# Sliding-window attention into an ELU feed-forward: four more groups transposed on TensorE, a split last chunk, and a new order of issue

## The chip, the core and the metric

The kernel runs on one core of one Trainium2 chip. The metric is the device time of one execution in microseconds (us); lower is better. A core has five engines that run their own instruction streams and meet only at semaphores: TensorE (PE; its weight loads are listed apart as PEld), VectorE (DVE), ScalarE (ACT), GpSimd (POOL) and SyncE (SP). Transfers are issued from the streams of SP, POOL and ACT and are carried by 16 DMA engines which all of them share.

## The reference

```python
scores = scale * np.matmul(q, k.transpose(0, 1, 3, 2))      # q, k, v: 8 x 8 x 576 x 64
mask = np.abs(pos[:, None] - pos[None, :]) <= 32
scores = np.where(mask, scores, -1000000000.0)
scores = scores - np.max(scores, axis=-1, keepdims=True)
attn = np.exp(scores)
attn = attn / (np.sum(attn, axis=-1, keepdims=True) + 1e-09)
attn_out = np.matmul(attn, v)
x = attn_out.transpose(0, 2, 1, 3).reshape(4608, 512)
h = x @ w_in                                                # w_in: 512 x 2048
g = np.where(h > 0.0, h, np.exp(np.minimum(h, 0.0)) - 1.0)
out = g @ w_out                                             # w_out: 2048 x 512
```

Inputs and output are fp32. Matmul operands on the chip are bf16, sums are fp32.

## The kernel before

**Units, groups, tiles, chunks.** The 8 x 576 query rows are cut into 72 units of 64 rows, nine to a batch. Attention works on groups of one or two units (list `G`; groups 0 to 8 cover units 0 to 15, and group i from 9 on covers units 2i-2 and 2i-1). The feed-forward works on tiles t of 2, 2, 2, 3, 4, 3 units and then seven tiles of 8 units (512 rows); tile 6 is made of groups 9 to 12, tile 7 of groups 13 to 16. Its output is made in 36 chunks c of 128 rows.

**What one group does.** Its queries and keys must stand transposed in SBUF, its values as blocks. Step `L` loads rows from DRAM (SP), `C`/`CV` cast them to bf16 (POOL; some of batch 0 on ACT and DVE), `TT` transposes k and q by a DMA (SP) from batch 2 on; batches 0 and 1 use TensorE (`T`, `TR`, with copies `TT` and `TTR` out of PSUM). Then `QK` (TensorE) makes the scores, `SM` (ACT) their exponential, `MK` (DVE) the mask, `AV` in two halves (TensorE) the product with v, `RN` (DVE) divides by the row sum and leaves x of the group in `xs`. From group 13 on, every second group is a "twin": its scores are made in the same `QK` step as those of the group before it, in the banks psT and psH.

**x must be transposed before the feed-forward.** Function `X` (L531) has two ways. For groups below `NC0 = 9` four TensorE transposes write psT (L544; step `XT`), and step `X` copies psT to the tile `xt` on ACT or DVE (L313 or L315, called from `XE`). For the others one DMA issued by SP does it (L540; step `X`). All groups of a tile must be in `xt` before its first `H`.

**The feed-forward.** `H` (L568) is four matmuls (16 or 8 for the small tiles) into one of three psH banks; `EX` (ACT, L577) is the exponential; `FF` clips it, on ACT (L589) or DVE (L591); `GG` (DVE, L597 or L600) takes the maximum with h, writes g and frees the bank. For the 8-unit tiles `FF` is on ACT for three of four. `Y` (L615) has four parts of four matmuls for each chunk; `YC` (ACT, L621) copies the sum to SBUF and frees the bank, `OUT` (L625) stores it from ACT's queue. `ypool` (L602) says in which bank a chunk is summed: psY alone for the first six, then psY and psT in turn, and four banks in turn for the last four chunks.

**What sets the order.** No loop nest does. Each step is given to a planner (`Plan`, L21) with an engine, a cost, dependences, the buffers it takes and frees, and a due time ("rank": about 4.0 per unit) to which the table `SHIFT` adds a number for each step named there. The planner walks through time, always starts the ready step of lowest rank on a free engine, and thereby fixes the order of issue of every engine. Table `ENG` moves single steps between ACT and DVE (or POOL). During its first 26 us the planner puts short dummy matmuls (`fill`, L514) into the gaps that it foresees on TensorE. At run time the engines follow that order strictly, each instruction waiting for the semaphores of what it needs.

**The start.** SP loads the rows of batch 0. POOL waits for block v2 of batch 0 (`WAIT`, L309), and then issues the loads of the second half of batch 0 (`LR`, L388, four transfers), of the weights (`WI`, L688, and `WO`, L693, four quarters each), and of batch 1 (`LR` 1).

Of the kernel before, what the change touches and what calls it, by code (L numbers as in the profile page):

```python
# [8 lines left out]
FP32 = mybir.dt.float32  # L9
# [181 lines left out]
def kernel(  # L191
# [9 lines left out]
    nc = tc.nc  # L201

    B, H, S, D = q.shape
# [3 lines left out]
    DM = H * D  # L207
# [14 lines left out]

    NBR = 2
    NTA = 5
    NC0 = 9
    NXT = 3
    NTW = 13
    NMA = 5
# [15 lines left out]
    yp = ctx.enter_context(tc.tile_pool(name="yp", bufs=3))  # L244
    psS_p = ctx.enter_context(tc.tile_pool(name="psS", bufs=1, space=PSUM))
    psO_p = ctx.enter_context(tc.tile_pool(name="psO", bufs=1, space=PSUM))
    psT_p = ctx.enter_context(tc.tile_pool(name="psT", bufs=1, space=PSUM))
# [63 lines left out]
    def copy(eng, dst, src):  # L311
        if eng is nc.scalar:
            nc.scalar.copy(dst, src)  # L313
        else:
            eng.tensor_copy(dst, src)  # L315
# [234 lines left out]
        copy(eng, dst, pt)  # L550


    es, ys = {}, {}

    def gcols(t):
        c = tiles[t][0] * QB % GC
# [44 lines left out]

    def ypool(c):  # L602
        if c < NCH - 4:
            return ((psY_p, "psY"), (psT_p, "psT"))[c % 2 if c >= 6 else 0]
        return ((psY_p, "psY"), (psO_p, "psO"), (psT_p, "psT"),
                (psS_p, "psS"))[c % 4]

# [8 lines left out]
                             rhs=w_out_sb[:, fo, :],  # L616
                             start=(fo == 0), stop=(fo == NFO - 1))

    def YC(c):
        y = yp.tile([128, DM], FP32, name="y", tag="y")  # L620
        nc.scalar.copy(y, ys.pop(c))  # L621
        ys[c] = y

    def OUT(c):
        nc.scalar.dma_start(out[c * 128:c * 128 + 128, :], ys.pop(c))  # L625

    NCH = N_TOK // 128
    sizes = [2, 2, 2, 3, 4, 3] + [8] * 7
# [2 lines left out]
    for t, n in enumerate(sizes):  # L631
# [8 lines left out]
    PER = 4.0  # L640
    LL, CC, XX = 36, 18, 14
    ENG = {
        ("CV", 0, 0, 0): "POOL", ("X", 4): "DVE", ("FF", 0, 4): "DVE", ("FF", 1, 0): "ACT",
        ("FF", 1, 8): "ACT", ("FF", 1, 12): "DVE", ("FF", 2, 0): "ACT", ("FF", 2, 4): "DVE",
        ("FF", 3, 6): "DVE", ("FF", 3, 10): "DVE", ("FF", 4, 0): "ACT", ("FF", 4, 4): "ACT",
        ("FF", 4, 6): "DVE", ("FF", 4, 8): "ACT", ("FF", 5, 2): "DVE"}
    SHIFT = {
        ("WI", 0): -17, ("WI", 1): -21, ("LR", 0, "k", 0): -31, ("LR", 0, "k", 1): -30,
        ("LR", 0, "q", 0): -29, ("LR", 0, "q", 1): -40, ("WI", 2): -21, ("WI", 3): -22,
        ("WO", 1): -23, ("WO", 2): -21, ("LR", 1, "k", 0): 2, ("WO", 3): -4, ("L", 0, "k",  # L650
        0): -32, ("L", 0, "k", 1): -33, ("L", 0, "q", 0): -40, ("L", 0, "v", 0): -35, ("L",
        0, "k", 2): -36, ("L", 0, "q", 1): -43, ("L", 0, "v", 2): -40, ("L", 0, "v", 4):
        -40, ("L", 1, "v", 0): -114, ("L", 1, "v", 1): -114, ("L", 1, "v", 3): -105, ("L",
        1, "v", 4): -117, ("L", 2, "k", 0): -6, ("TT", 2, 0): -138, ("L", 2, "k", 1): -6,
        ("TT", 2, 1): -5, ("TT", 2, 2): -13, ("TT", 3, 0): -4, ("TT", 3, 2): -10, ("L", 3,
        "k", 3): -6, ("TT", 3, 3): -7, ("L", 3, "k", 4): -6, ("TT", 3, 4): -16, ("L", 4,
        "k", 0): -6, ("L", 4, "k", 1): -6, ("TT", 4, 2): -40, ("TT", 4, 3): 8, ("TT", 4, 4):
        -17, ("L", 5, "k", 2): -6, ("TT", 5, 2): -11, ("L", 5, "k", 4): -6, ("TT", 5, 4): 1,
        ("TT", 6, 0): -30, ("TT", 6, 1): -8, ("L", 6, "v", 2): -4, ("TR", 1, "k", 0): 166,
        ("TR", 1, "k", 1): 174, ("TR", 1, "k", 2): 168, ("TR", 1, "q", 0): 169, ("TR", 1,  # L660
        "q", 1): 191, ("TR", 1, "q", 3): 158, ("QK", 3): -64, ("QK", 5): 187, ("XT", 7): 13,
        ("AV", 8, 0): 11, ("XT", 8): 55, ("X", 9): 17, ("QK", 10): 46, ("AV", 10, 0): 32,
        ("AV", 10, 1): 88, ("X", 10): 14, ("RN", 11, 0): 60, ("X", 11): 7, ("X", 14): -10,
        ("X", 16): -48, ("X", 17): 17, ("X", 18): -3, ("X", 19): 10, ("SM", 20, 0): -48,
        ("SM", 22, 0): -43, ("AV", 22, 0): 77, ("AV", 22, 1): 104, ("QK", 23): 41, ("X",
        23): 15, ("H", 0, 12): 81, ("H", 2, 0): 117, ("H", 2, 12): -98, ("GG", 2, 12):
        -2044, ("H", 3, 0): 140, ("H", 3, 2): 81, ("H", 3, 8): 186, ("H", 3, 12): 141, ("H",
        3, 14): 103, ("H", 4, 0): -34, ("H", 4, 2): -22, ("H", 4, 4): -18, ("H", 4, 14): 33,
        ("H", 5, 0): 21, ("H", 5, 2): 39, ("H", 5, 4): 19, ("FF", 5, 4): 81, ("GG", 5, 4):
        63, ("H", 5, 6): 57, ("H", 5, 10): 84, ("H", 5, 12): 13, ("H", 6, 0): 104, ("H", 6,  # L670
        11): -162, ("H", 7, 4): -158, ("H", 7, 10): -73, ("H", 8, 3): -74, ("EX", 8, 8): 49,
        ("EX", 9, 5): 17, ("Y", 0, 3): 100, ("Y", 1, 0): 152, ("Y", 1, 2): 164, ("Y", 3, 1):
        111, ("Y", 4, 1): 30, ("Y", 4, 3): 41, ("Y", 5, 0): 57, ("Y", 8, 3): -75, ("Y", 9,
        1): -191, ("Y", 9, 2): -68, ("Y", 11, 0): -79, ("Y", 11, 2): -47, ("Y", 12, 1):
        -140, ("Y", 13, 1): -67, ("Y", 14, 1): 34, ("Y", 14, 3): 90, ("Y", 15, 0): 116,
        ("Y", 15, 2): -18}
    RING, XBT = 2.8, 1.33
    LEAD = 36.0

# [200 lines left out]
    for i in range(NG):  # L880
        r = prank(i)
# [100 lines left out]
    for c in range(NCH):  # L982
# [16 lines left out]
        deps = [("Y", c, NQ - 1)]  # L999
        if c >= 3:  # L1000
            deps.append(("OUT", c - 3))
        P.op(("YC", c), "ACT", 0.6, r, deps, lambda c=c: YC(c),
             rel=(ypool(c)[1], 1))
        P.op(("OUT", c), "ACT", 0.42, r, [("YC", c)],
# [34 lines left out]
```

## Time and profile before

| what | value |
|---|---|
| median of 5 runs | 321.97 us (320.23 to 324.64) |
| the profiled execution, its own time | 319.84 us |
| its span, first to last instruction | 318.10 us |
| PE busy / PEld busy | 306.6 us (96%) / 169.3 us |
| ACT busy / DVE busy / POOL busy | 211.0 / 193.4 / 113.8 us |
| queue 1 (SP's loads and transposes), share of 16 engines | 64.8% |
| DMA transposes of x (L540), k and q (L332) | 28, median 3.3 us to landing; 30, 4.3 us |
| mean granted TensorE clock | 0.995 |

"Busy" adds up the times in which an engine has an instruction in work. Matmuls overlap one another, so a busy PE can still lose time, and the spacing between starts says more than the duration of one. The same holds for ACT: an instruction listed at 0.60 us can be followed by the next after 0.5. The 1.74 us between the span and the execution's own time lie before the first and after the last instruction. Times in the views count from the start of the span.

### The profile page before, as it was taken

To read this page: it belongs to the slowest core of one execution; us is meant where nothing else is said; L and a number is where in the kernel's file an instruction comes from. 1 tells how busy PE (TensorE), PEld (TensorE's weight loads), DVE (VectorE), ACT (ScalarE), POOL (GpSimd) and SP (SyncE) were. 2 spreads that over 40 slices of the span, in tenths; PEclk is the share of its full clock that TensorE was granted. 3 is DMA by queue.
4 is the path that set the end of the run, shared out by engine and by line. 5 is a ranking of instruction groups with operands and counts; after the bars stand their busy time and mean duration, and the time that the engine had idled before them with its cause. 6 is when DMAs were issued, how large, how long until landed. Compare 5 with 4: busy or idle time off the path is not lost.

```text
span 318.1 us, 7590 instructions
## 1 busy us (share of the span) xinstructions
PE 306.6 (96%) x2935; PEld 169.3 (53%) x2935; DVE 193.4 (61%) x414; ACT 211.0 (66%) x358; POOL 113.8 (36%) x166
## 2 busy tenths in 40 slices
PE   7899999999999997999999999999999999999995
PEld 5578776477754443444444544444454545444442
DVE  5147956779765797484658656758474848444300
ACT  2359754679765987676878638788777786676711
POOL 4980029956652355564265656412100000000000
PEclk9799999999999999999999999999999999999999
DMA  8999999999999999999999999998611111100121
GB/s 166 206 207 207 207 223 224 254 195 216 201 201 214 194 181 199 214 213 204 205 234 192 242 188 192 220 174 180 141 50 53 49 52 49 52 33 33 61 74 66
DMA packets 153636, 51.42 MB, mean 162 GB/s; under 512 B 143104, under 2 KB 148992, under 8 KB 153600
## 3 DMA queue, kind: packets, MB, share of 16 engines
q1 hardware_dynamic: 142304, 35.53, 64.8%
q0 software_dynamic: 6112, 5.96, 11.4%
q10 hardware_dynamic: 5184, 9.44, 9.1%
q8 instruction: 23, 0.38, 0.5%
q14 instruction: 13, 0.11, 0.1%
HBM read 36.70 MB, written 9.44 MB: 145 GB/s over the span
## 4 chain that ended last, share of the span: by engine, by line
PE 80%; DMA 8%; ACT 4%; POOL 3%; DVE 2%; issue 1%; SPq 0%; ACTq 0%; POOLq 0%
PE psH L568 33%; PE psY L615 21%; PE psT L615 15%; DMA w_out_sb<-in_moe_w_out_dram 5%; PE psO L501 5%; DMA xt<-xs 2%; PE psS L444 2%; ACT e L577 2%; ACT f L589 1%; DMA st<-in_v_dram 1%; POOL vw L315 1%; PE psS L615 1%; PE psO L615 1%; POOL w_in_sb L688 1%; DVE g_sb L597 1%
## 5 line engine op out<-in xcount | busy, mean ns | idle before, releaser
L568 PE MATMUL psH<-xt,w_in_sb 128*128 128x512 bf16 (+3 forms) x832 | 147.1, 313 | 3.5 <-DMA xt<-xs 2.0
L577 ACT ACTIVATE e<-psH 128x512 f32<-128x512 f32 (+1 forms) x148 | 86.1, 584 | 57.7 <-PE psH L568 50.9
L597 DVE SCALAR_TENSOR_TENSOR g_sb<-f,psH 128x512 bf16<-128x512 bf16 (+1 forms) x105 | 70.4, 673 | 57.3 <-ACT f L589 51.2
L568 PEld LDWEIGHTS <-w_in_sb 128*128 128x128 bf16 x832 | 69.2, 98 | 52.7 <-issue 2.6
L315 POOL CAST vw<-st 64x512 bf16<-64x512 f32 (+3 forms) x108 | 70.5, 653 | 52.0 <-DMA st<-in_v_dram 38.4
L615 PEld LDWEIGHTS <-g_sb 128*128 128x128 bf16 x576 | 53.3, 98 | 57.4
L615 PE MATMUL psY<-w_out_sb,g_sb 128*128 128x512 bf16 x320 | 80.8, 379 | 0.0
L589 ACT ACTIVATE f<-e 128x512 bf16<-128x512 f32 (+1 forms) x105 | 65.2, 621 | 3.1
L615 PE MATMUL psT<-w_out_sb,g_sb 128*128 128x512 bf16 x224 | 56.8, 379 | 0.0
L315 POOL CAST cb<-sp 128x1024 bf16<-128x1024 f32 (+1 forms) x30 | 31.9, 1064 | 57.3 <-DMA sp<-in_q_dram 56.7
L501 PEld LDWEIGHTS <-pm 128*128 128x128 bf16 x576 | 25.1, 97 | 15.8 <-DVE xs L528 5.8
L528 DVE TENSOR_TENSOR xs<-psO,rc 128x256 bf16<-128x256 f32 (+1 forms) x71 | 30.1, 424 | 2.4
L600 DVE TENSOR_TENSOR g_sb<-psH,f 128x512 bf16<-128x512 f32 (+1 forms) x43 | 28.7, 668 | 3.8 <-DVE f L591 0.5
L501 PE MATMUL psO<-vw,pm 128*128 128x65 bf16 x552 | 28.7, 193 | 0.6 <-DVE pm L488 0.3
L591 DVE TENSOR_SCALAR f<-e 128x512 bf16<-128x512 f32 (+1 forms) x43 | 19.2, 447 | 11.2 <-ACT e L577 10.8
L526 DVE RECIPROCAL rc<-psO 128x4 f32<-128x4 f32 (+1 forms) x71 | 12.6, 178 | 17.0 <-PE psO L501 15.5
L468 ACT ACTIVATE pu<-psS 128x1024 bf16<-128x1024 f32 (+1 forms) x20 | 19.9, 996 | 3.1 <-PE psS L444 3.0
L483 DVE TENSOR_TENSOR pm<-pu,masks 128x1024 bf16<-128x1024 bf16 (+1 forms) x21 | 15.6, 746 | 5.1 <-ACT pu L468 4.8
L621 ACT COPY y<-psY 128x512 f32<-128x512 f32 x20 | 11.6, 578 | 7.9 <-PE psY L615 7.9
L444 PEld LDWEIGHTS <-qk 64*128 64x128 bf16 x576 | 9.8, 95 | 9.3 <-issue 9.0
L488 DVE TENSOR_TENSOR pm<-pu,masks 128x512 bf16<-128x512 bf16 x22 | 12.8, 621 | 2.3 <-ACT pu L468 2.0
L621 ACT COPY y<-psT 128x512 f32<-128x512 f32 x14 | 8.1, 577 | 8.2 <-PE psT L615 8.2
(61 smaller groups left out, 130.2 us busy)
## 6 DMA issues: line engine op xcount, KB each, us to landing
out_dram<-y ACTq DMA_DIRECT2D x36, 256.0 KB, 2.9
sp<-in_q_dram SPq DMA_DIRECT2D x26, 256.0 KB, 5.1
sp<-in_k_dram SPq DMA_DIRECT2D x26, 256.0 KB, 4.6
st<-in_v_dram SPq DMA_DIRECT2D x24, 256.0 KB, 5.4
st<-in_v_dram SPq DMA_DIRECT2D x16, 192.0 KB, 4.5
w_in_sb<-in_moe_w_in_dram POOLq DMA_DIRECT2D x4, 512.0 KB, 11.9
w_out_sb<-in_moe_w_out_dram POOLq DMA_DIRECT2D x4, 512.0 KB, 17.4
sp<-in_k_dram SPq DMA_DIRECT2D x6, 128.0 KB, 4.3
```

Source lines behind the costliest of these rows:

```text
L315: eng.tensor_copy(dst, src)
L468: nc.scalar.activation(pu.rearrange("p x a s c -> p (x a) s c")[:, :, 0:n], live.pop(("S", i)).rearrange("p x a s c -> p (x a) s c")[:, :, ...
L501: nc.tensor.matmul(o[:, j, :], lhsT=p[:, HP * (h % 2) + h // 2, s * QB:s * QB + 128], rhs=vw[b % NVB][:, qb, h, :], start=(s == 0), stop=( ...
L528: nc.vector.tensor_mul(live["X", i][0:n, g * HP:(g + 1) * HP, :], o[0:n, :, 0:D], rb)
L568: nc.tensor.matmul(ps[:, f], lhsT=w_in_sb[:, do, (fo + f) * 128:(fo + f + 1) * 128], rhs=xts[t][:, do, :], start=(do == 0), stop=(do == ND ...
L577: nc.scalar.activation(e, ps, AX.Exp)
L589: nc.scalar.activation(f, e, AX.Relu, bias=1.0, scale=-1.0)
L591: nc.vector.tensor_scalar(f, e, -1.0, 0.0, ALU.add, ALU.min)
L597: nc.vector.scalar_tensor_tensor(g_sb[:, fo:fo + pack(t), gcols(t)], f, -1.0, ps, ALU.mult, ALU.max)
L600: nc.vector.tensor_tensor(g_sb[:, fo:fo + pack(t), gcols(t)], ps, f, ALU.max)
L615: nc.tensor.matmul(ps, lhsT=g_sb[:, fo, gc:gc + 128], rhs=w_out_sb[:, fo, :], start=(fo == 0), stop=(fo == NFO - 1))
L621: nc.scalar.copy(y, ys.pop(c))
```

## The change

There are three edits.

1. `NC0` goes from 9 to 13: x of groups 9 to 12 (all of tile 6) is transposed by TensorE and copied out of psT by ACT, where one DMA each did it. Chunks 6 and 7 now use psY, since `ypool` starts to alternate at chunk 8.
2. The last chunk (c = 35) is copied out of PSUM in two column halves, the first by ACT and stored from ACT's queue, the second by DVE and stored from SP's queue.
3. `ENG` and `SHIFT` are replaced, so that every engine's order of issue is new. The two tables name other steps, and other amounts.

```diff
-    NC0 = 9
+    NC0 = 13
...
-    es, ys = {}, {}
+    es, ys, yo = {}, {}, {}
...
-            return ((psY_p, "psY"), (psT_p, "psT"))[c % 2 if c >= 6 else 0]
+            return ((psY_p, "psY"), (psT_p, "psT"))[c % 2 if c >= 8 else 0]
...
-    def YC(c):
-        y = yp.tile([128, DM], FP32, name="y", tag="y")
-        nc.scalar.copy(y, ys.pop(c))
-        ys[c] = y
-
-    def OUT(c):
-        nc.scalar.dma_start(out[c * 128:c * 128 + 128, :], ys.pop(c))
+
+    def YC(c, half=None):
+        if c not in yo:
+            yo[c] = yp.tile([128, DM], FP32, name="y", tag="y")
+        w = slice(0, DM) if half is None else slice(half * DM // 2, (half + 1) * DM // 2)
+        copy(nc.vector if half else nc.scalar, yo[c][:, w], ys[c][:, w])
+
+    def OUT(c, half=None):
+        w = slice(0, DM) if half is None else slice(half * DM // 2, (half + 1) * DM // 2)
+        (nc.sync if half else nc.scalar).dma_start(
+            out[c * 128:c * 128 + 128, w], yo[c][:, w])
...
     ENG = {
-        ("CV", 0, 0, 0): "POOL", ("X", 4): "DVE", ("FF", 0, 4): "DVE", ("FF", 1, 0): "ACT",
-        ("FF", 1, 8): "ACT", ("FF", 1, 12): "DVE", ("FF", 2, 0): "ACT", ("FF", 2, 4): "DVE",
-        ("FF", 3, 6): "DVE", ("FF", 3, 10): "DVE", ("FF", 4, 0): "ACT", ("FF", 4, 4): "ACT",
-        ("FF", 4, 6): "DVE", ("FF", 4, 8): "ACT", ("FF", 5, 2): "DVE"}
+        ("CV", 0, 2, 0): "ACT", ("CV", 0, 2, 1): "ACT", ("CV", 0, 2, 2): "DVE", ("CV", 0, 3,
+        2): "DVE", ("TTR", 1, "k", 0): "ACT", ("TTR", 1, "q", 1): "DVE", ("TTR", 1, "q", 2):
+        "ACT", ("X", 7): "DVE", ("FF", 1, 8): "ACT", ("FF", 2, 4): "DVE", ("FF", 4, 0):
+        "ACT", ("FF", 4, 4): "ACT", ("FF", 4, 8): "ACT", ("FF", 4, 12): "ACT", ("FF", 5, 0):
+        "DVE", ("FF", 5, 6): "DVE", ("FF", 5, 10): "DVE"}
     SHIFT = {
...
+        ("WI", 0): -41, ("WI", 1): -54.7, ("LR", 0, "k", 0): -56, ("LR", 0, "k", 1): -56,
+        ("LR", 0, "q", 0): -72, ("LR", 0, "q", 1): -93, ("WI", 2): -94, ("WI", 3): -44,
...
+        -19, ("X", 17): 16.04, ("QK", 19): -92, ("SM", 19): 10, ("AV", 19, 1): -65, ("AV",
+        20, 0): -136, ("AV", 20, 1): -105, ("QK", 21): 70, ("AV", 21, 0): -86, ("QK", 23):
+        -107, ("SM", 24, 0): 42, ("H", 2, 0): 135, ("H", 3, 0): 234, ("H", 3, 2): 156, ("H",
...
+        if c == NCH - 1:
+            for h in range(2):
+                P.op(("YC", c, h), ("ACT", "DVE")[h], 0.35, r, deps,
+                     lambda c=c, h=h: YC(c, h), rel=(ypool(c)[1], 0.5))
+                P.op(("OUT", c, h), ("ACT", "SP")[h], (0.42, 0.62)[h], r, [("YC", c, h)],
+                     lambda c=c, h=h: OUT(c, h), dma=(("A", 8, 45), ("S", 8, 45))[h])
+            continue
```

In the order that results, first as it was and then as it is:

- POOL: `WAIT`, `CV`, four `LR`, `WI` 1, 0, 2, 3; now `WAIT`, `WI` 2, four `LR`, `WI` 1, 0, 3, and the casts of v2 and of block v0 have gone to ACT and DVE.
- TensorE's start: 65 fills in eight places, first `H` is (0, 4); now 70 fills in ten places, first `H` is (0, 8), and two of the four `TR` of batch 0 come after it.
- Between the first `H` of tile 6 and that of tile 7: 16 `H`, parts 0 to 2 of `Y` 8, two double `QK`, five half `AV`; now 16 `H`, all of `Y` 7, parts 0 to 2 of `Y` 8, two double `QK`, ten half `AV`.
- SP: the four transposes `X` 9 to 12 are gone from between the loads of batch 3, and loads and transposes of batch 4 follow closer. `QK` 19, the first of batch 4, stood after `Y` 10 part 0 and now stands after `Y` 8 part 3.

## The prediction

> **What bounds the kernel now.** I read the page first (TensorE busy for 306.6 of 318.1 us), then cut the span at marks of TensorE's stream: first `H`, first `Y`, first `H` of tiles 4, 6 and 7, first `Y` of the last four chunks.
>
> ```profile
> core 0: us, PE busy (x) PEld busy (x) DVE busy (x) ACT busy (x) POOL busy (x), PEclk, DMA share, GB/s
> 0.00:22.49 22.49, 18.54 (x261) 13.93 (x262) 9.79 (x30) 8.05 (x12) 17.46 (x37) 0.92 1.14 192
> 22.49:37.90 15.41, 15.10 (x288) 13.60 (x286) 11.71 (x28) 12.15 (x22) 0.74 (x1) 1.00 1.24 207
> 37.90:66.28 28.38, 27.65 (x407) 17.12 (x405) 18.79 (x42) 15.77 (x29) 18.96 (x27) 1.00 1.10 228
> 66.28:98.67 32.39, 32.24 (x390) 22.22 (x387) 23.96 (x56) 22.94 (x42) 16.72 (x23) 1.00 1.19 207
> 98.67:121.32 22.65, 19.83 (x187) 9.61 (x183) 18.10 (x37) 20.26 (x35) 10.10 (x13) 1.00 1.05 183
> 121.32:300.58 179.26, 179.26 (x1357) 86.69 (x1357) 109.88 (x222) 128.02 (x217) 49.79 (x67) 1.00 0.73 141
> 300.58:318.10 17.52, 13.97 (x65) 6.17 (x63) 1.14 (x2) 3.77 (x7) 0.00 (x0) 1.00 0.21 76
> ```
>
> From 121.3 us to the tail TensorE is never idle: nothing can be gained there but by doing less. What can be had lies before, most of it in the fifth row, tile 6, the only one where ACT's busy time (20.3) is above TensorE's (19.8). TensorE's waits in that row, and the longest of them with the transfer it waited for (view of SP's queue, then of PE):
>
> ```profile
> PE psH L568 <- DMA xt<-xs: 2.0, 1, 2.0
> PE psH L568 <- DVE g_sb L597: 0.7, 2, 0.4
> ...
> 115.72 1.73 SPq L540 DMA_TRANSPOSE xt<-xs  x1
> ...
> 121.32 1.90 PE L568 MATMUL psH<-xt,w_in_sb 128*128 128x512 bf16 x8 [2.00 <-DMA xt<-xs]
> ```
>
> Tile 7 could not begin before x of group 16 had landed, 5.6 us after its issue.
>
> For the work of a stage I count steps in TensorE's order and price each by the distance between starts: `H` of 512 columns or `Y` 0.863 us, half `AV` 0.242, `QK` 0.30 or double 0.572.
>
> **Part 1: four groups on TensorE.** Added: 16 transposes and four copies. The row that is the same operation:
>
> ```profile
> 62.02 0.39 PE L544 MATMUL psT<-ident,xs 128*128 128x128 bf16 x4
> 62.24 0.41 PE L501 MATMUL psO<-vw,pm 128*128 128x65 bf16 x8
> ...
> L313 ACT COPY xt<-psT 128x512 bf16<-128x512 bf16 x7 | 4.1, 582 | 1.9 <-PE psT L544 1.9
> ```
>
> The next step starts 0.22 us after the four transposes, so four groups cost 4 x 0.22 = **+0.9 us**, all on the bounding engine. A rule speaks against this: the Trainium skill, "TensorE: Matmul & The Clock Gate", Part 4 (PE-mode transpose), gives about 275 ns for one 128x128 bf16 transpose inside a kernel, an estimate of 16 x 0.275 = 4.4 us. The trace shows overlapped starts, so I take 0.9. The copies, 4 x 0.58 us, fall on ACT between 78 and 99 us, where it was busy for some 6 of 10 us: hidden while ACT isn't behind. The last, of group 12, gates the first `H` of tile 6. Only `Y` 6 part 3 (0.86) lies between its transposes and that `H`, and the copy needs about 0.9: 0.1 at most.
>
> Removed: four transfers whose landing no one waited for (group 12's landed at 95.3, tile 6 began at 98.7). Their absence alone gains nothing, but SP spent 6.4 us issuing them, and all of batches 3 and 4 behind them in SP's queue moves up by about that much.
>
> **Part 2: the order, stage by stage.**
>
> *Tile 6 (fifth row).* Before: 16 `H` 13.8, three parts of `Y` 2.6, two double `QK` 1.1, five half `AV` 1.2: 18.8 us of work took 22.65, so 3.85 are lost. ACT has 16 exps and 12 relus here. In the timeline an exp is followed by its relu after 0.63 us and that by the next exp after 0.54, and a lone exp by its successor after 0.48. So 12 x 1.17 + 4 x 0.48 = 15.9, and with 3.7 for the softmax exps 19.7 us: more than TensorE's 18.8. After: four parts of `Y` and five half `AV` more, 23.4 us of TensorE for 20.5 of ACT, with a `Y` copy added. The engine that was behind is now ahead. The wait on x goes too: between group 16's second `AV` half and tile 7 lay 5.1 us of work where the way from `AV` to landed x took 7.4 (113.9 to 121.3); in the new order there are 9.1. Late next is `GG` behind the softmax of groups 17 and 18: counting engine by engine, `H` 13 and 14 wait some 0.5 together. I leave 0.65 lost: 0.65 - 3.85 = **-3.2 us**. Bounds: -3.6 (0.3 lost, as in tile 7: 29.9 for 29.6), and -1.8 if only the x wait goes.
>
> *Tiles 4 and 5 (fourth row).* 31.1 us of work took 32.4, 1.3 lost. Now all eight relus of tile 4 are on ACT, two more than before, and g of (4, 6) is made late: the second part of `Y` 4 waits for it, I count 0.5. `QK` 13 keeps psT for group 14, and group 11's transposes wait for ACT to free it, 0.1. **+0.2 us**, between -0.5 and +2: by plain durations ACT has 12.3 us for TensorE's 10.4 here, by distances about as much as TensorE.
>
> *From the first `Y` to tile 4 (third row).* 25.9 us of work took 28.4. The number is unchanged. The stalls between the transposes of batch 1 should go, the one before `Y` 3 (0.5) stays behind `SM` 6: **-0.3**, between -1 and +0.5.
>
> *The start (first two rows).* The loads of k0 and k1 of batch 0 have the same bytes ahead of them within 64 KB, so `QK` 0 stays near 13.3. POOL sends the third weight quarter ahead of the `LR` loads. In the trace those loads began to move 2.9 us after issue, at 11.5; the quarter would begin at some 10.3, when k1's bytes are nearly through, so it delays only v3, v4 and the `LR` (which land 2 us before they are needed). The casts moved from POOL stand where ACT and DVE idle for 2 to 3 us; one, of v3 on DVE, delays a `GG` by 0.6 that nobody waits for yet. Ahead of `AV` there are 3 more fills (0.3) and ahead of `TR` five that wait for `RN`. In return one `H` runs before two `TR`. By this chain the first `Y` comes at 38.1, for 37.9: **+0.2**. What may change this is the clock:
>
> ```profile
> 10.00:11.00 1.00, 0.57 (x6) 1.00 1.33 203
> 11.00:12.00 1.00, 1.00 (x6) 0.52 1.33 214
> 12.00:13.00 1.00, 1.00 (x7) 0.50 1.33 194
> 13.00:14.00 1.00, 1.00 (x5) 0.50 1.30 212
> ```
>
> It was halved from 11.0 to 14.5 us, after 3.4 us in which TensorE was idle for 1.4. There the eight fills ran at 0.21 us apart, not 0.11, and `QK` 0 took 1.39, not 0.87. The new order has 12 fills in those 3.4 us where one was, but waits as long for k0: I get 61% busy for 58, and take the halved clock again. If it stays whole, `QK` 0 comes at 12.1 and the first `Y` at 36.8, 1.3 us earlier than by my chain. If it is halved for another such stretch, 0.8 later.
>
> *After tile 7.* No loss before, same steps now, `QK` 21 and 23 closer together: 0 (to +0.7).
>
> **Part 3: the tail.** Before:
>
> ```profile
> 314.59 0.59 ACT L621 COPY y<-psS 128x512 f32<-128x512 f32 x1 [2.87 <-PE psS L615]
> 315.21 0.34 ACTq L625 DMA_DIRECT2D out_dram<-y  x1
> ```
>
> Were the halves parallel, 0.40 us (between the 0.375 of ACT's 128x256 copy and the 0.49 of its exp of 384 columns) would replace 0.59: -0.2. But both halves are one PSUM bank. The Trainium skill, "PSUM — Partial Sum Buffer", PSUM bank collisions, says that two engines must not access one bank and the same partitions at once, reads included, and asks for a semaphore between them. No row shows a collision; the changed program has that semaphore: DVE's copy waits for ACT's copy, not for TensorE. So 0.40 + 0.1 + 0.4 (DVE's casts of 128x512 and 128x128 take 0.66 and 0.29) = 0.9 for 0.59, less perhaps 0.1 for a half-size store: **+0.2 us**, not -0.2.
>
> **Sum.** +0.9 - 3.2 + 0.2 - 0.3 + 0.2 + 0.2 = **-2.0 us**, against the profiled execution's 319.84 (a span of 318.10): 317.8. The median shown is 2.1 above that execution; on it, **320.0 us**.
>
> **Rivals.**
>
> - *The clock stays whole at the start.* For it: twelve fills in the deciding stretch. Against: 58% busy was not enough. -2.0 - 1.3 = -3.3, **318.7 us**; with the low bound of tile 6 and of the third row (another -1.1) 317.6.
> - *The bound only moves.* ACT is given four copies and two relus, and tiles 4 and 5 lose their upper bound (+2.0 for +0.2), while tile 6 gains only the wait on x (-1.8 for -3.2): -2.0 + 1.8 + 1.4 = +1.2, **323.2 us**. Against it: the distances between ACT's starts.
> - *Slower: keys of batch 4 too late.* `QK` 19 moves from 133.4 to about 122 and needs three transposes (L332), which landed by 127.9. I expect them at 119, since SP saves 6.4 us and one pair of loads with its v block (3.4) goes behind. If the removed transfers buy nothing, because the casts on POOL or the shared DMA engines (share above 1 there) set the pace, they land at 127.9 and TensorE stands for 5.5 us: -2.0 + 5.5 = +3.5, **325.5 us**. It decides from the point where they land after 122, and costs over 1% from 127.5.
> - *The change doesn't do what it says* in the tail; that is in the sum.
>
> **How the numbers follow.** Forecast 0.55 (its own range 318.5 to 321.5), whole clock 0.22, moved bound 0.13, late keys 0.10. About 1% is what a measurement of this kernel can tell from no change, so the limits are 318.75 and 325.2. Faster: 0.12 of the forecast, 0.15 of the whole clock, and 0.06 for losses of the first 98 us that vanish altogether: 0.33. Slower: 0.09, the late keys. Same: 0.58. Range: 316.6 (whole clock with its low bounds, and 1 us for the spread of medians) to 323.2.
>
> **What the changed profile would show.** Right: no wait of TensorE on `xt<-xs`; first `H` of tile 6 to first `H` of tile 7 in about 24 us; transposes 0.22 apart from what follows; the first `Y` near 38; DVE's half copy after ACT's. Wrong: a halved clock missing at 11 us, `Y` 4 waiting over a microsecond on `g_sb`, `QK` 19 waiting on a DMA, or a stall after 122 us, where I price nothing.

## The result

The changed kernel takes 323.58 us (median of 36 runs, 321.44 to 326.93), the kernel before 321.59 (71 runs beside them): a ratio of 1.0068, with a 95% interval of 1.005 to 1.0085. It is 0.7% slower, where 320.0 us was forecast, and lies outside the range given. Medians are over all executions; ratios leave out those that took over 1.5% longer than the fastest of the same kernel. The profiled execution took 322.95 us with a span of 321.2, 3.1 us more than that of before. The medians differ by 2.0 us, so sizes read from these two executions say where time is lost, and less well how much on the whole.

The changed kernel's span, cut at the same marks of TensorE's stream as in the prediction (first `H`; first `Y`; first `H` of tiles 4, 6 and 7; first `Y` of the last four chunks):

```profile
core 0: us, PE busy (x) PEld busy (x) DVE busy (x) ACT busy (x) POOL busy (x), PEclk, DMA share, GB/s
0.00:21.22 21.22, 18.84 (x213) 14.04 (x214) 10.39 (x32) 7.88 (x12) 12.52 (x29) 1.00 1.12 187
21.22:38.19 16.97, 16.73 (x345) 15.06 (x340) 12.02 (x30) 13.84 (x25) 2.43 (x4) 1.00 1.24 206
38.19:66.39 28.20, 27.53 (x408) 16.79 (x406) 18.60 (x39) 16.59 (x31) 18.16 (x26) 1.00 1.13 222
66.39:95.86 29.47, 29.20 (x366) 21.29 (x363) 22.66 (x53) 24.08 (x43) 17.51 (x23) 1.00 1.12 211
95.86:120.71 24.85, 24.09 (x238) 12.18 (x237) 19.46 (x43) 20.28 (x35) 12.03 (x16) 1.00 1.10 187
120.71:303.48 182.77, 179.86 (x1347) 86.19 (x1344) 111.04 (x221) 128.66 (x219) 48.37 (x64) 1.00 0.68 137
303.48:321.20 17.72, 13.97 (x65) 6.17 (x63) 1.56 (x3) 3.56 (x7) 0.00 (x0) 1.00 0.20 74
```

Tile 6 (fifth row) became what was forecast: TensorE is busy for 24.09 of 24.85 us, and tile 7 begins 0.6 us earlier than before although more work lies ahead of it. The loss is in the sixth row, the one for which the prediction put nothing (0 to +0.7): TensorE had no gap there before, and now 2.9 us of them. The longest of TensorE's waits in the whole execution, without those of the dummy matmuls at the start (engine, line, and what it waited for; us in total, times, longest):

```profile
PE psO L501 <- DVE xs L528: 2.2, 3, 1.7
PE psS L444 <- DMA qk<-cb: 0.7, 1, 0.7
PE psH L568 <- DMA xt<-xs: 0.5, 1, 0.5
```

The wait on keys (`qk`, L444) lies in tile 6; 2.0 of the first line's 2.2 us, and all of the last line, lie in the sixth row. The wait of 2.0 us on `xt<-xs` ahead of tile 7 is gone, but `xt<-xs` is there again, and the longest wait is that of an `AV` (L501) on `xs` (L528). The timeline around it shows why (first SP's queue at group 20, then all engines at group 26):

```profile
146.71 1.21 SPq L540 DMA_TRANSPOSE xt<-xs  x1
...
183.92 0.63 SPq L289 DMA_DIRECT2D sp<-in_k_dram  x1
184.59 0.64 SPq L289 DMA_DIRECT2D sp<-in_q_dram  x1
185.27 0.62 SPq L289 DMA_DIRECT2D st<-in_v_dram  x1
185.99 2.70 SPq L540 DMA_TRANSPOSE xt<-xs  x2
...
189.77 0.42 DVE L528 TENSOR_TENSOR xs<-psO,rc 128x256 bf16<-128x256 f32 x1 [1.90 <-DMA xt<-xs]
190.24 0.29 PEld L501 LDWEIGHTS <-pm 128*128 128x128 bf16 x8 [2.23 <-DVE xs L528]
190.25 0.42 PE L501 MATMUL psO<-vw,pm 128*128 128x65 bf16 x8 [1.74 <-DVE xs L528]
...
191.30 0.60 PEld L568 LDWEIGHTS <-w_in_sb 128*128 128x128 bf16 x4 [0.26 <-DMA xt<-xs]
```

Group 26 needs one of three `xs` buffers, and the one due is held until `X` 23 has been transferred (it landed at 189.67). `AV` of group 23 had ended at 178.7 and that of group 24 at 182.5, but SP issued their transfers at 186.0 and 187.5, behind two `TT` and three loads of batches 6 and 7. `X` 24 landed at 191.25 and the first `H` of tile 9, which needs it, began at 191.36. `X` 20 is the same on a smaller scale: its `AV` ended at 141.0, it was issued at 146.71 and landed at 149.30, and the first `H` of tile 8 began at 149.34, 0.7 us late.

By the steps of the prediction, each as the difference of the two profiled executions:

| step | forecast, us | measured, us |
|---|---|---|
| start, to the first `Y` | +0.2 | +0.3, but with unlike clocks (below: +1.5 to +1.9 with like ones) |
| first `Y` to tile 4 | -0.3 | -0.2 |
| tiles 4 and 5, beyond their work | +0.2 | +0.4 |
| tile 6, beyond its work | -3.2 | -2.5 |
| 16 transposes on TensorE | +0.9 | +0.9 |
| tile 7 to the tail, beyond its work | 0 | +4.0 |
| tail | +0.2 | +0.2 |
| sum | -2.0 | +3.1 |

"Beyond its work" is as in the prediction: the stage less its steps times their pitches (a pitch is the distance between starts). In the sixth row the steps come to 177.2 us after and 177.7 before, of 182.77 and 179.26, so 5.6 and 1.6 us are lost. The +4.0 is 0.7 in tile 7, 2.4 in tile 8, 0.6 in tile 9 and 0.3 in tile 10. The +0.2 of the tail is not its split copy, as the run with the whole chunk shows below.

### The profile page after: what moved, and what is told of

Same layout as the page of the kernel before. It is cut to its first block, busy times and chain, and to the rows that moved or that the text cites. A ratio compares the mean times of both kernels' runs of the same rounds, so it can differ in the third digit from the quotient of the medians.

```text
span 321.2 us, 7642 instructions
## 1 busy us (share of the span) xinstructions
PE 310.2 (97%) x2956; PEld 171.7 (53%) x2956; DVE 195.7 (61%) x416; ACT 214.9 (67%) x367; POOL 111.0 (35%) x160
## 3 DMA queue, kind: packets, MB, share of 16 engines
q1 hardware_dynamic: 140272, 35.14, 61.7%
## 4 chain that ended last, share of the span: by engine, by line
PE 79%; DVE 6%; ACT 4%; DMA 4%; SPq 3%; issue 2%; ACTq 0%; DVEq 0%
PE psH L568 31%; PE psY L615 20%; PE psT L615 11%; PE psO L501 5%; PE psO L514 2%; ACT e L577 2%; PE psS L444 2%; DMA xt<-xs 2%; DVE g_sb L597 2%; PE psH L398 2%; DVE xs L528 1%; DMA sp<-in_q_dram 1%; PE psH L342 1%; PE psS L615 1%; PE psO L615 1%
## 5 line engine op out<-in xcount | busy, mean ns | idle before, releaser
L597 DVE SCALAR_TENSOR_TENSOR g_sb<-f,psH 128x512 bf16<-128x512 bf16 (+1 forms) x107 | 71.9, 674 | 64.4 <-ACT f L589 56.6
L615 PE MATMUL psY<-w_out_sb,g_sb 128*128 128x512 bf16 x336 | 85.5, 379 | 0.0
L315 POOL CAST vw<-st 64x512 bf16<-64x512 f32 (+3 forms) x102 | 66.4, 652 | 43.0 <-DMA st<-in_v_dram 33.8
L589 ACT ACTIVATE f<-e 128x512 bf16<-128x512 f32 (+1 forms) x107 | 66.4, 622 | 3.1
L615 PE MATMUL psT<-w_out_sb,g_sb 128*128 128x512 bf16 x208 | 52.6, 379 | 0.0
L315 POOL CAST cb<-sp 128x1024 bf16<-128x1024 f32 (+1 forms) x30 | 32.6, 1089 | 56.0 <-DMA sp<-in_q_dram 50.4
L501 PEld LDWEIGHTS <-pm 128*128 128x128 bf16 x576 | 25.0, 97 | 20.2 <-DVE xs L528 9.5
L528 DVE TENSOR_TENSOR xs<-psO,rc 128x256 bf16<-128x256 f32 (+1 forms) x71 | 30.1, 424 | 4.8 <-DMA xt<-xs 2.4
L501 PE MATMUL psO<-vw,pm 128*128 128x65 bf16 x552 | 28.7, 193 | 3.1 <-DVE xs L528 2.2
L600 DVE TENSOR_TENSOR g_sb<-psH,f 128x512 bf16<-128x512 f32 (+1 forms) x41 | 27.5, 671 | 3.2
L483 DVE TENSOR_TENSOR pm<-pu,masks 128x1024 bf16<-128x1024 bf16 (+1 forms) x21 | 16.8, 798 | 2.4 <-ACT pu L468 1.6
L444 PEld LDWEIGHTS <-qk 64*128 64x128 bf16 x576 | 9.8, 95 | 8.5 <-issue 6.9
L514 PE MATMUL psO<-ident 128*128 128x252 bf16 x70 | 11.6, 319 | 2.2 <-POOL ident masks.py:199 1.4
L488 DVE TENSOR_TENSOR pm<-pu,masks 128x512 bf16<-128x512 bf16 x22 | 11.2, 549 | 2.9 <-ACT pu L468 2.2
```

What stands on the lines that cost most here:

```text
L501: nc.tensor.matmul(o[:, j, :], lhsT=p[:, HP * (h % 2) + h // 2, s * QB:s * QB + 128], rhs=vw[b % NVB][:, qb, h, :], start=(s == 0), stop=( ...
L514: nc.tensor.matmul(live["W"][:, 260:512].rearrange("p (a c) -> p a c", a=2), lhsT=ident, rhs=rhs, start=True, stop=True)
L528: nc.vector.tensor_mul(live["X", i][0:n, g * HP:(g + 1) * HP, :], o[0:n, :, 0:D], rb)
L589: nc.scalar.activation(f, e, AX.Relu, bias=1.0, scale=-1.0)
L597: nc.vector.scalar_tensor_tensor(g_sb[:, fo:fo + pack(t), gcols(t)], f, -1.0, ps, ALU.mult, ALU.max)
L600: nc.vector.tensor_tensor(g_sb[:, fo:fo + pack(t), gcols(t)], ps, f, ALU.max)
```

## The experiments

Ratios are to the kernel before, with a 95% interval. Where an edit is shown as a list of steps, the planner's order was kept and only the steps marked were moved, added or taken out. Where the order of one kernel is joined to the start of the other, the whole order is written out as a list.

**The place in SP's queue.**

```diff
 SP:  X17  TT(4,3)
+     X20
      L(5,k,2)  L(5,v,2)  TT(4,4)
-     X20
 ...
      X21  X22
+     X23
      TT(5,4)
+     X24
      TT(6,1)  L(6,k,4)  L(7,v,1)
-     X23  X24
```

> The changed kernel with three transfers placed earlier in SP's queue and nothing else moved: X of group 20 ahead of the loads L(5,k,2), X of 23 ahead of TT(5,4), X of 24 ahead of TT(6,1). Theory S (the new loss after tile 7 is the place of these transfers in SP's queue: their groups were done 5 us before their issue): the first H of tile 8 no longer waits (0.7 us), the second AV half of group 26 no longer waits for an xs buffer and the first H of tile 9 not for X24 (1.9 us together): 2.6 us less than the changed kernel, 321.0 on the median where it has 323.6, ratio to the kernel before 0.998. Theory D (the DMA engines are full, so what is brought forward only pushes the loads and TT behind it, and QK of batch 5 or 6 waits instead): 0 to 0.7 us less, ratio 1.004 to 1.007.

Measured: 320.77 us, ratio 0.9983 (0.9962 to 1.0004); the changed kernel's interval lies wholly above that. SP's queue, where three transfers (X 21 to 23) now stand together and the fourth is issued 3.4 us earlier:

```profile
177.54 4.04 SPq L540 DMA_TRANSPOSE xt<-xs  x3
181.62 2.38 SPq L332 DMA_TRANSPOSE qk<-cb  x1
184.09 1.22 SPq L540 DMA_TRANSPOSE xt<-xs  x1
```

From the first `H` of tile 8 to that of tile 9 the loss fell from 2.9 to 0.95 us, before tile 8 from 1.0 to 0.4; no wait of TensorE on `xt<-xs` is left, and nothing pushed back turned up as a new wait. Theory S holds. The gain is less sure in size: 1.9 and 2.8 us against the changed kernel's two results (322.70, in the run repeated below, and 323.58), but 1.4 us against the two kernels measured beside this one with the transfers in their old places (322.12 and 322.24, the next run and the one with the whole tail).

The place alone does not make the loss; the queue must also run late. The profiled execution of the kernel with the whole tail has the changed kernel's order up to the last chunk, and issues the same transfers earlier, `X` 20 and `X` 23 by more than 3 us (the second line is `X` 23 and 24):

```profile
143.51 1.71 SPq L540 DMA_TRANSPOSE xt<-xs  x1
182.58 4.81 SPq L540 DMA_TRANSPOSE xt<-xs  x2
```

There `AV` 26 waited 0.23 us and neither tile 8 nor tile 9 waited for x; tile 8 lost 1.05 us. In the two profiles of the changed kernel and in that of the four buffers `AV` 26 or tile 9 waited 1.7 to 2.4 us. Why the queue runs earlier in one execution than in another was not found.

**The ring of buffers.**

```diff
-    xsp = ctx.enter_context(tc.tile_pool(name="xsp", bufs=3))
+    xsp = ctx.enter_context(tc.tile_pool(name="xsp", bufs=4))
```

> The changed kernel with four xs buffers for three, order untouched. Theory R (the ring of xs buffers costs the time: RN of group 26 had to wait for X23): the wait of 1.7 us ahead of AV of group 26 goes and the kernel is 1.7 to 1.9 us faster than the changed one, ratio to before 1.001. Theory S: that wait goes too, but the first H of tile 9 needs X24, which lands at about 191.3 as before since its place in SP's queue is the same; TensorE waits there instead: 0 to 0.3 us less, ratio 1.006 to 1.007.

Measured: 322.12 us, ratio 1.0024 (1.0001 to 1.0048). The time lies between the two forecasts; its interval overlaps that of the repeated changed kernel (1.0025 to 1.0076) and ends just below that of the first result, so the times alone do not decide. The trace does: the wait of `AV` 26 is gone, and the same time is lost 3 us later, ahead of tile 9, on the transfer itself.

```profile
189.90 0.42 PE L501 MATMUL psO<-vw,pm 128*128 128x65 bf16 x8
190.15 1.03 PE L615 MATMUL psY<-w_out_sb,g_sb 128*128 128x512 bf16 x4
193.56 0.60 PE L568 MATMUL psH<-xt,w_in_sb 128*128 128x512 bf16 x2 [2.38 <-DMA xt<-xs]
```

The buffer was where the delay showed, not where it came from. (The profiled execution took 325.48 us; the place of the wait is read from it, not its size.)

**What makes SP late.** In the changed kernel SP is issuing for 25 of the 27 us from 95 to 122. Over the whole execution its issues take longer than the shortest of their kind: a transposing transfer 1.57 us in the median against 1.22 (L332), a `v` load 1.07 against 0.45 (the shortest with all 128 rows). The next kernel loads half of `v`'s heads and uses them twice, so its output is not the reference's.

```diff
+        hh = H // 2 if nm == "v" and b > 1 else H
-            out=t[r:r + n].rearrange("p (h d) -> p h d", h=H),
-            in_=SRC[nm][b].rearrange("h s d -> s h d")[lo:lo + n])
+            out=t[r:r + n].rearrange("p (h d) -> p h d", h=H)[:, 0:hh],
+            in_=SRC[nm][b].rearrange("h s d -> s h d")[lo:lo + n, 0:hh])
```

> The changed kernel with the v loads of batches 2 to 7 fetching four of the eight heads, and the casts taking those four twice, so that SP issues as many instructions and POOL casts as much; the output is therefore not the reference's. It tells why SP's queue runs late. If the bytes in flight hold SP up (its issues take 1.4 times their shortest time): its queue runs 3 to 4 us earlier by 120 us, the waits of QK of group 17, of tile 8 for X20 and of AV of group 26 for X23 go, and the kernel is 2 to 3 us faster than the changed one, ratio about 0.998. If the number of issues holds it up: X16, X20 and X23 are issued within 1 us of where they were, and the time is within 0.6 us of the changed kernel's, ratio 1.004 to 1.007.

Measured: 320.46 us, ratio 0.9981 (0.9964 to 0.9998). `X` 16 in the queue of this kernel, and then in that of the changed one:

```profile
111.79 1.19 SPq L549 DMA_TRANSPOSE xt<-xs  x1
113.07 3.00 SPq L332 DMA_TRANSPOSE qk<-cb  x2
```

```profile
117.15 1.22 SPq L540 DMA_TRANSPOSE xt<-xs  x1
118.46 2.65 SPq L332 DMA_TRANSPOSE qk<-cb  x2
```

With as many issues but less in flight the queue is 5.4 us earlier (in five executions with the changed kernel's queue up to there, `X` 16 was issued between 114.7 and 118.5), and every wait of TensorE on a transfer after the start is gone. Bytes and packets both fell by a tenth (queue 1: 35.14 MB in 140272 packets, now 31.60 in 126448), so the run does not tell which of the two counts; it does tell that the number of issues is not what holds SP back. An issue taken out of the queue can then free less than its own duration.

**The transposes alone.** The order of before, with `XT` 9 to 12 put into TensorE's list a few steps behind their `AV`, the copies into ACT's, and `X` 9 to 12 taken out of SP's.

```diff
-    NC0 = 9
+    NC0 = 13
 PE:  Y(4,2)  + XT9   H(5,14)   ...   Y(5,0)  + XT10  Y(5,1)
      Y(5,3)  + XT11  H(5,10)   ...   Y(6,2)  + XT12  Y(6,3)
-SP:  X9  X10  X11  X12
```

> The kernel before in its own order, with X of groups 9 to 12 on TensorE and an ACT copy, each at most a few steps after its AV halves, and their four transfers gone from SP's queue; nothing else moved. By the prediction's steps: +0.9 us of TensorE; SP gets on earlier, so X of group 16 is issued when its group is done (about 1 us earlier) and lands 1 to 2 us earlier, which takes that much of the wait of 2.0 us ahead of tile 7: -1.1 to 0.0 us, ratio 0.9965 to 1.000. If the four transposes cost more than their pitch (stalls of psT behind ACT's copies): +0.5 to +2 us, ratio 1.0015 to 1.006.

Measured: 320.02 us, ratio 0.9962 (0.9939 to 0.9986): faster than before, by slightly more than forecast. `X` 16 landed at 118.64 for 121.27 and tile 7 did not wait for it. So the first part of the change is sound, and the loss comes with the new order. How much of the gain is the transposes' own is less clear, since the clock differs too (last section).

**The new order without them.** The changed kernel, `X` 9 to 12 by transfer again, where their transposes stood.

```diff
-    NC0 = 13
+    NC0 = 9
-PE:  XT9  XT10  XT11  XT12
+SP:  TT(2,3) X9 L(3,k,2) ... L(3,v,3) X10 L(3,k,4) ... TT(3,2) X11 L(4,k,0) X12 L(4,v,0)
```

> The changed kernel in its order, with X of groups 9 to 12 by transfer again: the transposes and copies are gone, four transfers stand in SP's queue where the transposes stood in the order. Theory S (SP's queue is what runs late): 0.9 us less of TensorE, but all of SP's queue from 79 us on about 5 us later, so that the keys of group 17 and of group 19, X20, X23 and X24 come later: 1 to 4 us more than the changed kernel, ratio 1.010 to 1.019. If the transposes themselves are the loss: 0.9 us less or more than that, ratio 1.004 or lower.

Measured: 332.51 us, ratio 1.036 (1.0326 to 1.0394), worse than any theory had it, and by another wait than those expected: one ahead of tile 6.

```profile
105.27 1.89 PE L568 MATMUL psH<-xt,w_in_sb 128*128 128x512 bf16 x4 [10.64 <-DMA xt<-xs]
```

`X` 12 was issued at 101.6, 9 us after the end of its `AV`, and landed at 105.2. TensorE's clock was also halved from 98.6 to 108.8 us, so that the first `H` behind the wait took 1.68 us to the next step and not 0.86. The new order asks for tile 6 at 95 us, which these transfers at these places cannot meet; other places were not tried.

**The start.** All instructions up to the first `Y` as in the kernel before (order, engines, fills), the changed order behind.

```diff
-POOL:  WI2  LR(q,1)  LR(q,0)  LR(k,0)  LR(k,1)  WI1  WI0  WI3 ...
+POOL:  LR(q,1)  LR(k,0)  LR(k,1)  LR(q,0)  WI1  WI0  WI2  WI3 ...
-PE:    ... TR(q,0) XT1 TR(q,1) H(0,8) TR(k,0) TR(k,1) H(1,8) QK2 H(0,4) ...
+PE:    ... TR(k,0) TR(k,1) XT1 TR(q,0) TR(q,1) H(0,4) QK2 H(1,4) H(0,0) ...
```

> The changed kernel with all instructions up to the first Y in the order and on the engines of the kernel before (weight loads, loads of batch 0, casts, fills, first H); all later ones as in the changed kernel. Theory T (the new start costs 1.9 us and not 0.2, since the third weight quarter goes ahead of the LR loads and of the two quarters needed first; it showed 38.2 us for the first Y with a whole clock, where the old order has 36.3 with a whole clock): first Y at 36.3 with a whole clock, 37.9 with the halved one, and 1.5 to 1.9 us less than the changed kernel, ratio 1.001. Rival (what is won at the start is lost again before tile 4, since the LR loads and the loads of batch 2 set that pace): 0 to 0.5 us less, first H of tile 4 still at 66.

Measured: 320.73 us, ratio 0.9991 (0.9969 to 1.0012), which is 1.9 to 2.5 us below the changed kernel's two results (1.0051 and 1.0068). The first `Y` came at 36.21, with a whole clock. Part of it is lost again: in the profiled execution (323.32 us) tile 6 waited where the changed kernel does not,

```profile
100.14 0.41 PE L444 MATMUL psS<-qk 64*128 64x64 bf16 x16 [2.14 <-DMA qk<-cb]
```

since TensorE was 2 us earlier and the keys of group 15 were not: they landed at 100.10 (97.86 in the changed kernel), and those of its twin, group 16, at 100.98 (98.73). The clock was then halved from 100.9 to 104.3 us.

The next run puts one move of this start, the place of the third weight quarter, into the kernel before.

```diff
 POOL:
+        WI2
         LR(q,1)  LR(k,0)  LR(k,1)  LR(q,0)  WI1  WI0
-        WI2
         WI3
```

> The kernel before with one move: the third weight quarter WI(2) ahead of the LR loads in POOL's queue, as the changed kernel has it; everything else in the order of the kernel before. The prediction's step (the quarter fits in behind k1 and delays only v3, v4 and the LR loads, which have 2 us to spare): 0 to 0.3 us. Theory T (it also delays everything behind it, the two quarters needed first too, by its own transfer of about 2.5 to 3 us): WI(1) lands at 22.9 instead of 20.3, the first H waits for it and the first Y comes 2 to 2.5 us later than in the kernel before with the same clock: +2 us, ratio 1.006.

Measured: 320.98 us, ratio 0.9996 (0.9973 to 1.0018). The trace does as theory T said (WI1 lands at 22.93, the first `Y` comes at 38.84 with a whole clock), the times do not follow. Two more kernels bear on this. The first is the mirror of the run with the old start: the changed start, and the order of before behind it.

```diff
-POOL, PE, ACT, DVE, SP up to Y(0,0): as before
+POOL, PE, ACT, DVE, SP up to Y(0,0): as in the changed kernel
```

> The mirror of the run with the old start: the kernel before with all instructions up to the first Y in the order and on the engines of the changed kernel, all later ones as in the kernel before. If the new start costs what the trace shows (first Y at 38.2 for 36.3 with a whole clock, 39.4 for 37.9 with a halved one) whatever follows: +1.3 to +1.9 us, ratio 1.004 to 1.006. If the order of the kernel before takes it up again, since its tile 7 waits 2.0 us for X16 anyway: -0.3 to +0.5 us, ratio 0.999 to 1.0015.

Measured: 322.10 us, ratio 1.0032 (1.0009 to 1.0056): the new start costs about 1.0 us in the old order too. The second is the changed kernel with the old start, in which the quarter alone is moved ahead.

```diff
 POOL (old start):
+        WI2
         LR(q,1)  LR(k,0)  LR(k,1)  LR(q,0)  WI1  WI0
-        WI2
```

> The changed kernel with the old start, but POOL's queue of the changed one in its main point: WI(2) ahead of the LR loads. If the place of this quarter is what the new start costs: as slow as the changed kernel, ratio 1.004 to 1.007. If it costs nothing here either, and the old start gains by its fills, casts and order of H: as fast as with the old start, ratio 0.998 to 1.001.

Measured: 321.55 us, ratio 1.0005 (0.9978 to 1.0033): inside the second forecast, and the first lies outside the interval. In both orders the quarter's place puts the first `Y` 2.4 to 2.6 us back in the trace, and the times by at most a part of that. So the new start as a whole costs about 1.0 us in the old order and about 2 in the new one, and the place of that quarter is a part of it at most. What the rest is (fills, casts, the order of `LR` and `H`) was not taken apart and stays open.

**The tail.** The last chunk whole, as before, in the changed kernel.

```diff
-        if c == NCH - 1:
+        if False:
             for h in range(2):
                 P.op(("YC", c, h), ("ACT", "DVE")[h], 0.35, r, deps,
```

> The changed kernel with the last chunk copied whole by ACT and stored whole on ACT's queue, as in the kernel before; the rest untouched. By the prediction's step on the tail (the second half copy waits for the first, 0.9 us for 0.59): 0.2 us less than the changed kernel. By its rival (two half copies side by side and two half stores): 0.2 us more. Both lie inside what the times can tell; the profile's stretch from the start of the last Y part to the end decides: 4.57 us by the first, 4.8 or more by the second.

Measured: 322.24 us, ratio 1.0029 (1.0012 to 1.0046). From the start of the last `Y` part to the end of the span it took 4.9 us with the whole chunk, 4.8 with the halves, 4.6 in the kernel before; to the last landing 3.7 in all three. So the split makes no difference: the 4.57 forecast for the whole chunk did not come, and the difference to the kernel before lies behind the last landing. What the times show here is the spread of the other waits. The changed kernel's tail is as the prediction described it, DVE's half beginning when ACT's is through:

```profile
317.49 0.37 ACT L313 COPY y<-psS 128x256 f32<-128x256 f32 x1 [2.87 <-PE psS L615]
317.89 0.34 ACTq L628 DMA_DIRECT2D out_dram<-y  x1
317.89 0.42 DVE L315 COPY y<-psS 128x256 f32<-128x256 f32 x1 [11.82 <-ACT y L313]
318.35 0.39 SPq L628 DMA_DIRECT2D out_dram<-y  x1
```

**The changed kernel again,** unchanged, measured beside the old start, the transfers put back, and the first joined version.

> The changed kernel itself once more, beside the three others of this call, so that they are compared on one chip. Every theory: ratio to the kernel before between 1.005 and 1.0085 again. If it comes out near 1.003, the small gains of the runs with four xs buffers and with the whole tail were a difference between chips and not of the edits.

Measured: 322.70 us, ratio 1.0051 (1.0025 to 1.0076).

**Versions that join the edits.** The first:

```diff
+start up to Y(0,0): as before
 SP:  L(4,v,0)
+     X13  TT(3,4)  TT(3,3)
      L(4,k,1)  L(4,v,1)
-     X13  TT(3,4)
      X14
-     TT(3,3)
+and X20, X23, X24 as in the first run; last chunk whole
```

> The changed kernel with four edits: the start of the kernel before, as in the run of the old start; X of 20, 23 and 24 earlier in SP's queue, as measured; X of 13 and the transfers TT(3,4) and TT(3,3), which QK of group 17 waited for (0.7 to 1.3 us), ahead of the loads L(4,k,1); the last chunk whole. Theories S and T together: -1.7, -2.2, -0.7 and 0: 4.6 us less than the changed kernel, about 319.0 us, ratio 0.992. If the gains are not independent, because an earlier TensorE meets the same SP queue: 2 to 3 us less, ratio 0.997 to 1.000.

Measured: 319.85 us, ratio 0.9961 (0.9937 to 0.9984): the gains are not independent. Its trace has 1.6 us of wait ahead of `QK` 15, on SP's queue. The next version takes that away, and splits the last chunk in another way: TensorE makes the left half of the columns in one PSUM bank, then the right half in another.

```diff
 SP:  L(3,v,3)
+     TT(3,1)  TT(3,2)
      L(3,k,4)  L(3,v,4)
-     TT(3,1)  TT(3,2)
+    def YH(part):
+        c, h = NCH - 1, part // 2
+        if part == 2:
+            HC(0)                       # ACT copies and stores the left half
+        if part % 2 == 0:
+            pool, nm = ((psS_p, "psS"), (psH_p, "psH"))[h]
+            ys[c, h] = pool.tile([128, DM // 2], FP32, name=nm, tag=nm)
+        for fo in range(8 * (part % 2), 8 * (part % 2) + 8):
+            nc.tensor.matmul(ys[c, h], lhsT=g_sb[:, fo, gc:gc + 128],
+                             rhs=w_out_sb[:, fo, h * 256:h * 256 + 256], ...)
```

> As the run with four edits (old start; X13, TT(3,4), TT(3,3), X20, X23, X24 earlier in SP's queue; ratio 0.996), and TT(3,1) and TT(3,2), for which QK of group 15 waited 1.6 to 2.1 us there, ahead of the loads of L(3,k,4); and the last chunk in two column halves in two PSUM banks. If that wait was due to the place in the queue: 1.6 us and 0.4 us less, ratio 0.990. If SP's queue simply has no more time to give and the wait turns up at QK of group 17 or 19: at most 0.5 us less, ratio 0.995.

Measured: 320.17 us, ratio 0.9951 (0.992 to 0.9982). The wait of `QK` 15 is gone and, after the start, no wait on SP's queue has come in its place, but the time is within 0.1% of the version without it, near the second forecast for another reason: tile 6 now waits 1.7 us for a `GG` of DVE, ahead of its 14th `H`. The tail works, since the left half is stored beside TensorE's work:

```profile
313.28 0.37 ACT L637 COPY y<-psS 128x256 f32<-128x256 f32 x1 [1.16 <-PE psS L630]
313.68 0.34 ACTq L638 DMA_DIRECT2D out_dram<-y  x1
315.02 0.37 ACT L637 COPY y<-psH 128x256 f32<-128x256 f32 x1 [1.37 <-PE psH L630]
315.43 0.34 ACTq L638 DMA_DIRECT2D out_dram<-y  x1
```

From the copy of the chunk before to the last landing it takes 5.63 us; the kernel before takes 6.07. The last version joins this tail to the transposes alone, in the order of before.

```diff
+NC0 = 13, XT9 to XT12 as in the run with the transposes alone
+last chunk by YH, as above
```

> The kernel before with X of groups 9 to 12 on TensorE in its own order (as in the run with the transposes alone, ratio 0.9962), and the last chunk computed as two column halves in two PSUM banks, the first half complete 1.7 us before the second, each copied and stored by ACT. Expected: the first half's copy and store lie beside TensorE, the last copy is 0.37 for 0.59 us and the last store 1.8 for 2.0 us: the last landing 0.4 us nearer to the start of the last Y part, ratio 0.995. If 256 columns cost TensorE more than half of 512: 0.2 to 0.5 us more instead.

Measured: 319.40 us, ratio 0.9940 (0.9914 to 0.9967), with 5.62 us for the tail. It has the lowest ratio here, though its interval overlaps those of the other joined versions and of the transposes alone. It lies 1.1 to 1.3% below the changed kernel's two results, and has none of the change's new order.

## Why the prediction was wrong

**The step that failed most** is that after tile 7: "No loss before, same steps now, `QK` 21 and 23 closer together: 0 (to +0.7)". It measured +4.0 us in the trace. With `X` 20, 23 and 24 earlier in SP's queue 1.3 of the 4.0 were left in the trace, and the time was 1.4 to 2.8 us less; what is left, in tiles 7 to 10, stays open. The prediction saw that an earlier TensorE makes the queue's landings late and followed this for the keys of `QK` 19, which came in time (forecast at 119, landed at 122.97, needed at 123.73). It did not ask the same of `X`, whose landings also gate `RN` three groups on and the first `H` of a tile. In the new order, `X` 24 stands behind two pairs of key loads more than before; it landed at 191.25, where it had landed at 186.26. SP's issues of `X` 23 and `X` 24 in the kernel before:

```profile
180.19 1.23 SPq L540 DMA_TRANSPOSE xt<-xs  x1
...
183.05 1.69 SPq L540 DMA_TRANSPOSE xt<-xs  x1
```

**A premise under it** was "SP spent 6.4 us issuing them, and all of batches 3 and 4 behind them in SP's queue moves up by about that much". By landing times it moved up by 3.2 us at the end of batch 3's loads, 4.9 at 107 us (L(4,v,1)), 3.7 at TT(4,0), and 0.5 at the end of batch 4's loads. The run with half of `v` shows why: the queue goes at the pace of what is in flight, not of its issues. The same queue took 0.7 us of the gain of tile 6, as the wait of `QK` 17 for TT(3,3), where the prediction had put the rest of the loss on `GG` alone. That step gave -2.5 for -3.2 us: right mechanism, size off by that wait.

**The step on the start,** +0.2 us, is too small: the start undone or put in alone moves the times by about 2 and 1 us. The forecast first `Y`, 38.1 us, was hit (38.19) by accident: it was worked out for a halved clock, and this execution had a whole one, with which the rival had it at 36.8. So the chain was 1.4 us short, and 1.3 with the lower clock of the repeated run (39.41). In the step, "it delays only v3, v4 and the `LR`" failed: the two weight quarters behind came 3 us later as well (WI1 at 23.0 for 20.3). But that alone doesn't account for the cost in time, as the two runs on the quarter show, and the cause within the start is not settled.

**The rivals.** "The clock stays whole at the start" happened in the profiled execution, without its gain. "Keys of batch 4 too late" named the right queue, but the wrong transfer and place. "The bound only moves" had 323.2 us, near the measured time, for another reason: tiles 4 and 5 lost 0.4 us and not 2.0.

**What was right**: the cost of the transposes by their pitch (0.9 us, and the run with them alone), the vanished wait ahead of tile 7, ACT no longer behind in tile 6, and the tail's two copies one after the other, with no gain. That the tail came out at the +0.2 forecast was luck: the split cost nothing that can be measured.

## What to carry to other kernels

An engine that gets ahead meets the next queue: when work moves earlier, every transfer that gates it has to be looked up in its queue against the new time of need, not only the one that was late before. Where a queue is held by what is in flight, an issue removed can give back less than its duration, and urgent small transfers belong ahead of loads that have time. A good part (here the transposes, 0.4% faster by themselves) is best measured apart from the new order that it comes with. One trace shows one execution: before a wait is called the cost of an order, a second trace of the same order should have it too.

## What the runs showed of the hardware

The halved clock at the start isn't a property of the kernel. The run with the transposes alone has the instructions of the kernel before up to 77 us; in its profiled execution the clock was whole where that of before was halved from 11.0 to 14.5 us, and the first `Y` came at 36.28 for 37.90.

(The last three figures of a row are the granted clock, the share of the DMA engines and GB/s.)

```profile
11.00:12.00 1.00, 1.00 (x11) 0.93 (x11) 0.00 (x0) 0.47 (x1) 1.00 (x2) 1.00 1.36 215
12.00:13.00 1.00, 1.00 (x22) 0.56 (x19) 0.00 (x0) 0.12 (x1) 1.00 (x2) 1.00 1.37 195
```

The changed kernel shows both too: its second profile, of the repeated run, has the lower clock (from 8.9 to 12.3 us, behind a wait of 1.8 us for a load) and the first `Y` at 39.41 for 38.19.

```profile
11.00:12.00 1.00, 1.00 (x7) 0.71 (x6) 0.71 (x2) 0.66 (x2) 1.00 (x2) 0.50 1.17 189
12.00:13.00 1.00, 1.00 (x9) 0.91 (x8) 0.73 (x2) 0.00 (x0) 1.00 (x3) 0.83 1.20 196
```

So with like clocks the new start is 1.9 us (whole) and 1.5 us (halved) later than the old.

The clock is also halved later on. In the run with the new start in the old order tile 7 waited 2.61 us for x, and eight matmuls behind the wait took 3.29 us, where eight took 1.90 in the kernel before:

```profile
123.86 3.29 PE L568 MATMUL psH<-xt,w_in_sb 128*128 128x512 bf16 x8 [2.61 <-DMA xt<-xs]
124.00:125.00 1.00, 1.00 (x3) 0.29 (x2) 0.00 (x0) 0.00 (x0) 0.89 (x3) 0.50 1.16 263
```

The old start in the new order (a wait of 2.14 us) and the transfers put back (10.64 us) show it too. In the kernel before, the clock stayed whole behind the wait of 2.0 us at the same place.

The mean granted clock of every execution is on record, and the times go with it. Of the executions that count for the ratios:

| kernel | clock 0.997 or more: number, median us | lower: number, median us |
|---|---|---|
| before | 26, 320.28 | 41, 321.70 |
| transposes alone, measured beside it | 19, 319.80 | 2, 321.48 |
| before, at another time | 23, 320.47 | 27, 321.79 |
| changed kernel again, measured beside it | 12, 322.60 | 4, 324.10 |

The changed kernel is slower by 2.1 us with a whole clock and 2.3 with a lower one, so the clock is not the cause of its loss. The transposes alone gain 0.5 us with a whole clock in both; the rest of their 1.4 us comes with a clock that was whole in 19 of 21 executions, and in only 26 of 67 of the kernel before. Whether it stays whole because the wait ahead of tile 7 is gone was not tested. What decides the clock of an execution was not found.
